# A new order of work and of later loads for a fused attention and gated MLP kernel on one core

## The chip, the core and the metric

The kernel runs on one core of one Trainium2 chip. The metric is device time in microseconds (us), the median over several executions. A core has a tensor engine (PE; its weight loads are listed as PEld), a vector engine (DVE), a scalar engine (ACT), a GpSimd engine (POOL) and a sync engine (SP). Here POOL issues nearly all loads and stores, SP issues the DMA transposes and the last stores. Each engine, and each of these DMA queues, works through its own list in order; semaphores hold an instruction until what it needs is there.

## The reference

```python
# q, k, v: (8, 8, 576, 64); beacon_k, beacon_v: (8, 8, 16, 64)
k_all = np.concatenate([beacon_k, k], axis=2)
v_all = np.concatenate([beacon_v, v], axis=2)
scores = q @ k_all.transpose(0, 1, 3, 2) / 8
causal[:, 16:] = np.triu(np.ones((576, 576), bool), k=1)   # the beacons are seen by all
a = softmax(np.where(causal, -1e9, scores))
x = (a @ v_all).transpose(0, 2, 1, 3).reshape(4608, 512)
out = ((x @ w1) * (x @ w2)) @ w3 @ w_out                    # w1, w2: 512x1024, w3: 1024x1024, w_out: 1024x512
```

Inputs and output are float32.

## The kernel before

The work is in float16 with float32 sums in PSUM. Two facts shape it. First, w3 and w_out are multiplied once into Wt (1024 x 512), so that the MLP is two products per token and one behind them. Second, there is no loop: the program is a list of 1,190 small steps, written out by hand or by a search in the string `ORDER` (line 62 on). A step is a name and its arguments; the last lines of the kernel walk the list and call the function of that name. The order in the string is therefore the order of every engine's own list and of every DMA queue. What the functions do not say, the semaphores that the framework adds do.

The steps, by the engine that they use. b is a batch image (0 to 7), c a chunk of 128 rows, t a pair of heads, h a half of the query blocks, g one of 13 groups of score blocks, mc a block of 512 tokens (0 to 8), kf and mt are blocks of 128 columns or tokens. n is always a PSUM bank, D and A name DVE and ACT, P, S and A the queue of a DMA.

Loads: `lq b c`, `lk b c`, `lv b c` load a chunk of q, k, v; `lkb b`, `lvb b` the beacons; `l1 c`, `l2 c` a quarter of w1, w2 (which serves kf 2c and 2c+1); `l3 r` an eighth of w3; `lo a` a quarter of w_out. They are issued by POOL (and cast to float16 on the way), except the first q and k, which come in float32 on SP and ACT.

Transposes of q and k: `cast`, then `tq`, `tk` (PE) and `eq`, `ek` (the copy out of PSUM, on D or A) in images 0 and 1 and most of 2; `Dq`, `Dk` (a DMA transpose on SP) in the rest and later. For w3: `t3 r` (PE), `e3 r` (copy), `f r a` (two products with w_out), `ew r` (copy into Wt). `tn`, `en` do the beacon keys of image 0.

Attention: `s b g n` (PE) writes a group of scores into a pair of banks, `exp b g n` (ACT) takes it out into a ring of 8 slots, `m b t h` (DVE) multiplies the diagonal blocks by a mask, `v b t h n` (PE) multiplies by the values with a column of ones behind them, `n b t h n` (DVE, two instructions: a reciprocal and a product) divides by the sum. `x b i n` and `ex b i e n` transpose the result through PE and a copy; `TX b i` does it by a DMA transpose on SP.

MLP: `a mc kf n` and `b mc kf n` (PE, four matmuls each), `ea` (copy of a on D or A into one of 3 buffers), `eb` (DVE, product), `o mc mt n` (PE, eight matmuls), `eo` (copy out on D or A into one of 8 buffers), `st mc mt` (the store). The last `o` is split into 384 and 128 columns.

`spin k n` issues k matmuls of zeros, to fill PE's time at the start. `consts` writes masks and zeros.

Two of these functions carry lines that the profile names: the four matmuls of `a` and `b` are line 580, the eight of `o` line 601.

```python
def load_rows(b, c, src, dst):          # lq from image 1 on: line 332 is the dma_start
    rows = min(P, S - c * P)
    nc.gpsimd.dma_start(
        dst[:rows, c], src[b, :, ds(c * P, rows), :].rearrange("h s d -> s h d")
    )
```

`lk` and `lv` issue at line 340, `l1` and `l2` at 390, `l3` at 399; `t3` is line 484, `f` 493, `s` 508, `exp` 518, `v` 539, `eb` 595. An image's q, k, v buffers are used again two images later, so a load of image b waits until the readers of image b-2 are done, and everything behind it on POOL waits with it.

Of the kernel before, what the change touches and what calls it, by code (L numbers as in the profile page):

```python
# [75 lines left out]
f 2 0 4; l1 2; ew 5 A 6; s 0 6 0; s 0 7 2; l3 7; exp 0 6 0; t3 1 6; lq 1 1 P; f 2 1 4; e3 1 D 6;
f 2 2 4; exp 0 7 2; lq 1 4 P; f 2 3 4; m 0 2 0; f 1 0 7; lq 1 0 P; ew 2 A 4; f 1 1 7; f 1 2 7;
lk 1 2 P; f 1 3 7; v 0 2 0 6; lk 1 3 P; ew 1 D 7; v 0 0 0 5; n 0 2 0 6; lk 1 4 P; s 0 8 0;
v 0 0 1 7; exp 0 8 0; n 0 0 0 5; s 0 9 2; s 0 10 4; n 0 0 1 7; lv 1 3; exp 0 9 2; v 0 1 0 6;
m 0 2 1; v 0 1 1 7; exp 0 10 4; n 0 1 0 6; l1 0; t3 7 3; tq 1 3 2; n 0 1 1 7; s 0 11 0; s 0 12 4;  # L80
lv 1 1; eq 1 3 A 2; v 0 2 1 6; e3 7 D 3; exp 0 11 0; l2 0; tq 1 1 7; m 0 3 0; f 7 0 3; n 0 2 1 6;
lq 2 1 P; v 0 3 0 2; exp 0 12 4; f 7 1 3; n 0 3 0 2; l1 1; tk 1 2 6; eq 1 1 A 7; f 7 2 3; m 0 3 1;
x 0 4 5; lv 1 2; x 0 0 4; ek 1 2 D 6; ex 0 4 A 5; tk 1 4 7; v 0 3 1 2; ex 0 0 D 4; ek 1 4 A 7;
l2 1; tk 1 3 6; n 0 3 1 2; f 7 3 3; ek 1 3 A 6; lv 1 4; tq 1 4 7; tq 1 0 5; ew 7 D 3; eq 1 4 A 7;
x 0 3 4; x 0 1 6; lq 2 0 P; eq 1 0 A 5; x 0 2 7; ex 0 3 D 4; ex 0 1 A 6; s 1 0 0; s 1 1 2; s 1 2 4;
ex 0 2 D 7; lv 2 0; exp 1 0 0; a 0 0 6; l2 2; exp 1 2 4; m 1 0 0; b 0 0 7; ea 0 0 D 6; lk 2 0 P;
exp 1 1 2; s 1 3 0; s 1 4 4; eb 0 0 7; tq 2 1 6; a 0 1 7; exp 1 3 0; eq 2 1 D 6; l1 3; m 1 0 1;
b 0 1 6; ea 0 1 D 7; l2 3; exp 1 4 4; s 1 5 2; s 1 6 0; s 1 7 4; m 1 1 0; eb 0 1 6; exp 1 5 2;
lk 2 2 P; b 0 3 7; exp 1 7 4; m 1 1 1; lq 2 2 P; v 1 0 1 6; v 1 1 0 3; n 1 0 1 6; lkb 2; exp 1 6 0;
v 1 1 1 5; lk 2 4 P; tq 2 0 4; n 1 1 0 3; v 1 0 0 6; eq 2 0 A 4; b 0 2 2; n 1 1 1 5; lk 2 3 P;  # L90
m 1 2 0; a 0 2 4; n 1 0 0 6; lv 2 3; v 1 2 0 5; ea 0 2 A 4; a 0 3 6; n 1 2 0 5; lk 2 1 P; eb 0 2 2;
ea 0 3 A 6; s 1 8 0; s 1 9 4; s 1 10 2; exp 1 8 0; eb 0 3 7; lq 2 3 P; a 0 7 6; lq 2 4 P;
exp 1 10 2; m 1 2 1; a 0 6 7; ea 0 7 D 6; lkb 3; Dk 2 0; exp 1 9 4; s 1 11 0; s 1 12 2; ea 0 6 D 7;
lq 3 1 P; tk 2 2 6; b 0 6 7; ek 2 2 D 6; exp 1 11 0; lv 2 4; m 1 3 0; lv 2 1; tk 2 4 6; v 1 3 0 5;
exp 1 12 2; eb 0 6 7; Dk 2 3; a 0 5 4; lq 3 2 P; n 1 3 0 5; ek 2 4 A 6; b 0 5 7; m 1 3 1;
ea 0 5 A 4; lv 2 2; v 1 3 1 6; eb 0 5 7; x 1 4 5; tk 2 1 4; n 1 3 1 6; x 1 0 7; lq 3 4 P;
v 1 2 1 3; ex 1 0 D 7; b 0 4 6; lk 3 2 P; ek 2 1 D 4; ex 1 4 D 5; tq 2 2 7; lk 3 1 P; n 1 2 1 3;
tq 2 4 4; b 0 7 5; eq 2 2 A 7; eq 2 4 D 4; lk 3 4 P; x 1 2 7; eb 0 7 5; x 1 1 4; lvb 2; ex 1 2 A 7;
x 1 3 3; Dq 3 1; a 0 4 2; ex 1 1 D 4; ex 1 3 A 3; lv 3 0; tq 2 3 7; ea 0 4 A 2; a 1 3 5; lq 3 3 P;
eq 2 3 D 7; eb 0 4 6; o 0 2 7; Dq 3 2; lvb 3; ea 1 3 A 5; lq 3 0 P; Dq 3 4; s 2 0 0; s 2 1 2;  # L100
s 2 2 4; eo 0 2 D 7; exp 2 0 0; lv 3 4; o 0 1 6; Dk 3 2; exp 2 1 2; m 2 0 0; st 0 2 P; exp 2 2 4;
o 0 0 7; m 2 0 1; Dk 3 1; eo 0 1 D 6; lk 3 3 P; lk 3 0 P; Dk 3 4; s 2 3 0; s 2 4 2; s 2 5 4;
eo 0 0 A 7; exp 2 4 2; lq 5 2 P; v 2 0 0 6; a 1 0 7; n 2 0 0 6; exp 2 5 4; v 2 0 1 3; ea 1 0 D 7;
lq 4 2 P; o 0 3 6; exp 2 3 0; m 2 1 1; Dq 3 3; lk 4 3 P; n 2 0 1 3; m 2 1 0; s 2 6 4; s 2 7 0;
s 2 8 2; lq 4 3 P; eo 0 3 D 6; exp 2 6 4; v 2 1 0 7; Dq 3 0; st 0 3 P; b 1 0 6; n 2 1 0 7;
exp 2 8 2; m 2 2 0; a 1 1 5; lk 4 2 P; eb 1 0 6; exp 2 7 0; v 2 2 0 7; m 2 2 1; b 1 1 6;
ea 1 1 A 5; n 2 2 0 7; lv 3 1; v 2 1 1 4; eb 1 1 6; a 1 2 7; Dk 3 3; n 2 1 1 4; lq 4 0 P; s 2 9 2;
s 2 10 0; s 2 11 4; exp 2 9 2; Dk 3 0; b 1 3 6; st 0 1 P; exp 2 11 4; m 2 3 0; a 1 4 3; eb 1 3 6;
lv 3 2; exp 2 10 0; v 2 3 0 2; m 2 3 1; b 1 4 6; ea 1 4 D 3; ea 1 2 A 7; v 2 2 1 5; n 2 3 0 2;
lq 4 4 P; a 1 6 7; eb 1 4 6; n 2 2 1 5; x 2 4 4; x 2 0 6; ex 2 4 A 4; a 1 5 3; lv 3 3; ex 2 0 D 6;  # L110
ea 1 6 D 7; b 1 6 6; ea 1 5 A 3; lk 5 3 P; s 2 12 0; s 3 0 4; s 3 1 2; eb 1 6 6; lk 4 0 P;
exp 2 12 0; Dq 4 2; b 1 2 7; lk 4 4 P; exp 3 1 2; v 2 3 1 6; Dk 4 2; lkb 4; eb 1 2 7; s 3 2 0;
s 3 3 2; st 0 0 P; exp 3 0 4; m 3 0 1; a 1 7 7; Dq 4 0; n 2 3 1 6; lv 4 4; exp 3 3 2; b 1 7 5;
m 3 0 0; lk 4 1 P; ea 1 7 D 7; Dk 4 3; exp 3 2 0; x 2 3 6; x 2 1 4; m 3 1 0; x 2 2 7; ex 2 3 D 6;
b 1 5 3; ex 2 2 A 7; Dq 4 4; ex 2 1 D 4; lq 4 1 P; eb 1 7 5; a 2 0 6; eb 1 5 3; Dq 4 3; s 3 4 0;
s 3 5 4; s 3 6 2; ea 2 0 A 6; exp 3 4 0; v 3 1 0 7; o 1 0 6; n 3 1 0 7; exp 3 6 2; exp 3 5 4;
m 3 2 0; v 3 0 1 7; eo 1 0 D 6; Dk 4 0; v 3 2 0 3; v 3 0 0 5; n 3 0 1 7; st 1 0 P; o 1 3 6;
n 3 2 0 3; Dk 4 4; n 3 0 0 5; m 3 1 1; s 3 7 0; s 3 8 2; s 3 9 4; lq 6 4 P; exp 3 7 0; eo 1 3 D 6;
a 2 2 7; lv 4 2; exp 3 8 2; v 3 1 1 6; st 1 3 P; ea 2 2 D 7; Dk 4 1; s 3 10 0; s 3 11 2; exp 3 9 4;
n 3 1 1 6; b 2 2 7; m 3 2 1; exp 3 11 2; a 2 3 6; Dq 4 1; m 3 3 0; eb 2 2 7; exp 3 10 0; v 3 3 0 5;  # L120
ea 2 3 D 6; b 2 1 4; lk 6 0 P; n 3 3 0 5; v 3 2 1 7; lq 5 4 P; m 3 3 1; TX 3 0; lk 5 1 P; b 2 0 6;
n 3 2 1 7; lvb 4; a 2 1 5; eb 2 0 6; TX 3 4; lv 4 3; o 1 2 7; ea 2 1 D 5; lv 4 1; eb 2 1 4;
lq 5 0 P; a 2 4 6; eo 1 2 D 7; lv 4 0; b 2 4 5; ea 2 4 D 6; st 1 2 P; o 1 1 7; eb 2 4 5; s 3 12 2;
s 4 0 0; s 4 1 4; eo 1 1 D 7; exp 3 12 2; Dk 5 3; b 2 7 6; st 1 1 P; exp 4 1 4; b 2 3 7; Dq 5 4;
exp 4 0 0; v 3 3 1 3; m 4 0 1; Dq 5 2; a 2 5 5; eb 2 3 7; lv 5 1; n 3 3 1 3; a 2 7 7; ea 2 5 A 5;
lk 5 4 P; Dq 5 0; m 4 0 0; lk 5 0 P; s 4 2 0; s 4 3 2; s 4 4 4; ea 2 7 A 7; exp 4 3 2; lq 5 3 P;
eb 2 7 6; TX 3 3; b 2 5 7; lkb 6; v 4 0 0 6; exp 4 4 4; m 4 1 0; a 2 6 3; TX 3 2; eb 2 5 7;
lk 5 2 P; exp 4 2 0; n 4 0 0 6; v 4 1 0 7; lv 5 0; b 2 6 5; TX 3 1; ea 2 6 D 3; lq 5 1 P;
v 4 0 1 6; n 4 1 0 7; Dk 5 1; lkb 5; s 4 5 0; s 4 6 2; eb 2 6 5; exp 4 5 0; lv 5 3; o 2 2 7;
n 4 0 1 6; Dk 5 4; exp 4 6 2; lv 5 2; m 4 1 1; s 4 7 4; s 4 8 0; s 4 9 2; eo 2 2 A 7; m 4 2 0;  # L130
exp 4 8 0; st 2 2 P; v 4 2 0 6; o 2 0 7; n 4 2 0 6; Dq 5 3; exp 4 7 4; m 4 2 1; exp 4 9 2;
v 4 1 1 6; eo 2 0 D 7; s 4 10 0; s 4 11 4; s 4 12 2; Dk 5 2; n 4 1 1 6; st 2 0 P; exp 4 10 0;
o 2 3 7; m 4 3 0; Dk 6 0; exp 4 11 4; exp 4 12 2; v 4 2 1 6; m 4 3 1; Dq 6 4; b 3 3 5; n 4 2 1 6;
eo 2 3 A 7; a 3 1 4; Dq 5 1; st 2 3 P; v 4 3 1 7; ea 3 1 D 4; Dk 5 0; a 3 4 6; n 4 3 1 7;
v 4 3 0 4; ea 3 4 A 6; TX 4 2; b 3 6 7; n 4 3 0 4; b 3 1 6; TX 4 0; a 3 3 4; eb 3 1 6; a 3 5 3;
# [562 lines left out]
```

## Time and profile before

| | |
|---|---|
| median of 4 runs | 291.82 us (291.66 to 292.3) |
| the profiled execution | 292.3 us; span from its first to its last instruction 290.6 us |
| busy: PE, DVE, ACT, POOL | 283.8, 174.4, 143.3, 133.9 us |
| granted TensorE clock | 1.00 |
| data moved | 39.32 MB read, 9.44 MB written, 168 GB/s over the span |

A span is the time between the first and the last instruction of the program; the time of a run is some 1.7 us longer. A busy time counts an engine's instructions without its waits; matmuls overlap, so that PE can be busy and yet slower than it could be. In the slices of the page the span is cut in 40 equal parts and each digit is a busy share in tenths. A line of a group has the source line, the engine, the operation, out<-in, and the count.

### The profile page before, as it was taken

The page shows a single profiled execution, that of the slowest core. Times are in us where ns is not written, and L with a number is a line of the kernel's source. Part 1 is how long each engine was busy: PE and PEld are TensorE (multiplying, and loading weights), DVE is VectorE, ACT ScalarE, POOL GpSimd, SP SyncE. Part 2 cuts the span into 40 slices and gives each one's busy share as a digit, 9 for nine tenths or more (in the row PEclk, how much of TensorE's full clock was granted, in tenths as well). Part 3 has the DMA queues.
Part 4 walks back from the last instruction along what each step waited for, and adds up shares of the span by engine and source line. Part 5 has one row for each costly group of instructions (what it writes and reads, how often), then busy time and mean ns, then how long its engine had stood idle before and what let it go on. Part 6 is the DMA issues. An engine that isn't in the chain of part 4 may idle for free.

```text
span 290.6 us, 7026 instructions
## 1 busy us (share of the span) xinstructions
PE 283.8 (98%) x2906; PEld 153.7 (53%) x2906; DVE 174.4 (60%) x377; ACT 143.3 (49%) x181; POOL 133.9 (46%) x187
## 2 busy tenths in 40 slices
PE   7999999999999999999999999999999999999994
PEld 2545675565556565555544555555545445444442
DVE  4356686884676788575563586546746746545621
ACT  3574689655665751578124546567191162110201
POOL 8769897798676267391096951820010011000000
PEclk9999999999999999999999999999999999999999
DMA  9999999999999999999999999999340015200034
GB/s 156 200 195 177 172 172 177 172 145 148 169 180 156 165 178 137 187 127 181 180 111 120 205 125 198 114 163 181 62 87 25 36 38 153 72 2 0 0 146 146
DMA packets 154512, 38.93 MB, mean 134 GB/s; under 512 B 144304, under 2 KB 150192, under 8 KB 154480
## 3 DMA queue, kind: packets, MB, share of 16 engines
q0 software_dynamic: 114800, 26.46, 110.6%
q1 hardware_dynamic: 39472, 11.72, 25.8%
q8 instruction: 23, 0.38, 0.6%
q10 hardware_dynamic: 208, 0.29, 0.4%
q14 instruction: 9, 0.07, 0.1%
HBM read 39.32 MB, written 9.44 MB: 168 GB/s over the span
## 4 chain that ended last, share of the span: by engine, by line
PE 90%; DMA 5%; POOL 3%; issue 1%; DVE 0%; POOLq 0%
PE one L580 44%; PE one L601 22%; PE one L539 10%; PE pair L508 9%; DMA xT<-in_moe_w_dram 5%; PE one L493 2%; PE one L428 1%; PE one L565 1%; POOL st L357 1%; PE one L484 1%; POOL xT L399 1%; POOL wo L402 0%; POOL q L332 0%; POOL k L377 0%; POOL b L369 0%
## 5 line engine op out<-in xcount | busy, mean ns | idle before, releaser
L580 PE MATMUL one<-xT,w 128*128 128x512 f16 x576 | 134.4, 379 | 0.0
L518 ACT ACTIVATE ring<-pair 128x1024 f16<-128x1024 f32 x104 | 99.0, 1028 | 32.5 <-PE pair L508 32.2
L580 PEld LDWEIGHTS <-w 128*128 128x128 f16 x576 | 52.5, 98 | 57.7 <-issue 2.5
L601 PE MATMUL one<-Wt,gT 128*128 128x512 f16 (+2 forms) x296 | 66.5, 373 | 0.0
L595 DVE TENSOR_TENSOR gT<-one,asb 128x512 f16<-128x512 f32 x72 | 48.8, 688 | 26.5 <-PE one L580 16.1
L300 ACT ACTIVATE asb<-one 128x512 f32<-128x512 f32 x34 | 20.4, 599 | 67.8 <-PE one L580 49.8
L615 POOL DMA_DIRECT2D out_dram<-st x27 | 15.3, 567 | 77.0 <-DVE st L302 38.5
L601 PEld LDWEIGHTS <-gT 128*128 128x128 f16 x296 | 27.3, 98 | 30.5 <-issue 0.9
L539 PEld LDWEIGHTS <-ring 128*128 128x128 f16 x960 | 35.8, 97 | 11.4 <-issue 1.1
L340 POOL DMA_DIRECT2D va<-in_v_dram x40 | 34.3, 862 | 13.1 <-PE one L539 9.2
L539 PE MATMUL one<-va,ring 128*128 128x65 f16 x960 | 38.4, 193 | 0.0
L340 POOL DMA_DIRECT2D k<-in_k_dram x35 | 29.8, 857 | 11.7 <-DMA kT<-k 9.2
L551 DVE TENSOR_TENSOR x<-one,rd 128x384 f16<-128x384 f32 (+1 forms) x64 | 31.4, 491 | 2.4 <-DVE rd L550 0.2
L302 DVE TENSOR_SCALAR asb<-one 128x512 f32<-128x512 f32 x38 | 26.1, 688 | 10.1 <-PE one L580 9.7
L332 POOL DMA_DIRECT2D q<-in_q_dram x35 | 30.2, 865 | 3.1 <-DMA qT<-q 1.0
L508 PE MATMUL pair<-qT,kT 64*128 64x80 f16 (+4 forms) x736 | 30.2, 225 | 0.0
L302 DVE TENSOR_SCALAR st<-one 128x512 f32<-128x512 f32 (+1 forms) x23 | 15.4, 672 | 20.6 <-PE one L601 20.5
L508 PEld LDWEIGHTS <-kT 64*128 64x128 f16 x736 | 19.9, 95 | 14.2 <-issue 11.9
L528 DVE TENSOR_TENSOR ring<-ring,MD 128x768 f16<-128x768 f16 x32 | 17.7, 552 | 11.0 <-ACT ring L518 11.0
L550 DVE RECIPROCAL rd<-one 128x6 f32<-128x6 f32 (+1 forms) x64 | 11.7, 182 | 14.9 <-PE one L539 14.6
L300 ACT ACTIVATE st<-one 128x512 f32<-128x512 f32 (+1 forms) x14 | 8.3, 596 | 23.9 <-PE one L601 23.7
L528 DVE TENSOR_TENSOR ring<-ring,MX 128x384 f16<-128x384 f16 x32 | 11.3, 353 | 11.7 <-ACT ring L518 11.7
(62 smaller groups left out, 134.4 us busy)
## 6 DMA issues: line engine op xcount, KB each, us to landing
out_dram<-st POOLq DMA_DIRECT2D x27, 256.0 KB, 5.4
q<-in_q_dram POOLq DMA_DIRECT2D x28, 128.0 KB, 7.3
va<-in_v_dram POOLq DMA_DIRECT2D x24, 128.0 KB, 6.9
k<-in_k_dram POOLq DMA_DIRECT2D x21, 128.0 KB, 6.5
xT<-in_moe_w_dram POOLq DMA_DIRECT2D x8, 256.0 KB, 6.4
w<-in_moe_w_dram POOLq DMA_DIRECT2D x8, 256.0 KB, 7.3
out_dram<-st SPq DMA_DIRECT2D x8, 256.0 KB, 2.0
wo<-in_moe_w_out_dram POOLq DMA_DIRECT2D x4, 256.0 KB, 7.0
```

Source lines behind the costliest of these rows:

```text
L300: nc.scalar.activation(dst, src, AF.Copy, scale=by)
L302: nc.vector.tensor_scalar(dst, src, by, None, ALU.mult)
L332: nc.gpsimd.dma_start(dst[:rows, c], src[b, :, ds(c * P, rows), :].rearrange("h s d -> s h d"))
L340: nc.gpsimd.dma_start(dst[ds(p0, rows), c], src[b, :, ds(s0, rows), :].rearrange("h s d -> s h d"))
L508: nc.tensor.matmul(shape(n, "pair")[:, hh, ds(col, w)], kT[ds(hh * 64, 64), t, ts(jt, P)], qT[ds(hh * 64, 64), t, ds(q0, w)],)
L518: nc.scalar.activation(held(b, g)[:, :, 0:GW], shape(n, "pair"), AF.Exp, scale=scale)
L528: nc.vector.tensor_tensor(blk, blk, msk, ALU.mult)
L539: nc.tensor.matmul(pv[:, 2 * at + hh, 0 : D + 1], held(b, g)[:, hh, ds(col, P)], va[:, jt, 2 * t + hh, 0 : D + 1], start=(jt == 0), stop=( ...
L551: nc.vector.tensor_tensor(x16s[b % NB2][:, ds(2 * h, ni), ts(t, P)].rearrange("p i (h d) -> p i h d", h=2), pv[:, 0 : 2 * ni, 0:D].rearran ...
L580: nc.tensor.matmul(bank(n), w12[:, kt, ds(i * DF + kf * P, P)], xT[:, kt, ds(mc * 512, 512)], start=(kt == 0), stop=(kt == NKT - 1),)
L595: nc.vector.tensor_tensor(gTs[mc % 2][:, kf, :], bank(n), asb[slot["asb", (mc, kf)]], ALU.mult)
L601: nc.tensor.matmul(bank(n)[:, 0:w], gTs[mc % 2][:, kf, ts(mt, P)], Wt[:, kf, ds(c0, w)], start=(kf == 0), stop=(kf == NFT - 1),)
```

## The change

Only the string `ORDER` changes. The steps stay the same, with their operands, but for three things: two spins more (24 instead of 22), the other engine for 96 of the casts and copies that may run on either DVE or ACT (of all 176, DVE has 100 before and 96 after), and the split last tile, which is mt 0 of block 7 instead of mt 3. The banks of many steps change too. The first 74 DMAs of POOL keep their order (up to `lvb 2`); the later loads, stores and DMA transposes, and the order of PE's, DVE's and ACT's steps from the start on, are new. The diff replaces 123 lines of the string by 123 others; these are the parts that the prediction speaks of.

```diff
 consts 0; lq 0 0 S; lk 0 0 A; l3 6; consts 1; spin 8 7; lq 1 2 P; l3 4; lo 1; lkb 0 P;
-cast 0 0 q D; lo 0; cast 0 0 k A; spin 3 7; tq 0 0 6; lkb 1; consts 2; eq 0 0 D 6; spin 1 7;
-tk 0 0 7; lq 0 1 P; t3 6 5; ek 0 0 A 7; lk 0 1 P; e3 6 D 5; spin 2 6; tq 1 2 6; l3 3; eq 1 2 D 6;
-spin 3 7; t3 4 7; lvb 0; e3 4 A 7; lo 2; spin 3 6; tn 0 6; en 0 D 6; spin 1 7; s 0 0 0; s 0 1 2;
...
-eq 0 1 A 5; spin 1 0; t3 3 3; lq 0 3 P; m 0 0 1; s 0 3 0; s 0 4 4; l3 5; e3 3 D 3; exp 0 3 0;
-f 6 2 6; lvb 1; f 4 2 7; exp 0 4 4; m 0 1 0; l3 2; tk 1 0 3; f 3 0 2; ek 1 0 D 3; f 3 1 2; t3 0 5;
-lq 0 2 P; f 3 2 2; e3 0 D 5; cast 0 2 k A; lk 1 1 P; s 0 5 0; f 0 0 4; exp 0 5 0; tk 0 2 5; lv 0 4;
-f 4 3 7; f 0 1 4; ek 0 2 A 5; m 0 1 1; l3 1; f 6 3 6; cast 0 3 k D; ew 4 A 7; f 3 3 2; lv 0 0;
-cast 0 3 q D; ew 6 D 6; tq 0 3 5; tk 0 3 7; eq 0 3 A 5; f 0 2 4; ew 3 D 2; lv 1 0; t3 5 6;
-ek 0 3 A 7; f 0 3 4; e3 5 D 6; lv 0 2; ew 0 A 4; t3 2 7; lv 0 3; f 5 0 6; e3 2 D 7; f 5 1 6;
...
-lq 3 1 P; tk 2 2 6; b 0 6 7; ek 2 2 D 6; exp 1 11 0; lv 2 4; m 1 3 0; lv 2 1; tk 2 4 6; v 1 3 0 5;
-exp 1 12 2; eb 0 6 7; Dk 2 3; a 0 5 4; lq 3 2 P; n 1 3 0 5; ek 2 4 A 6; b 0 5 7; m 1 3 1;
...
-eq 2 3 D 7; eb 0 4 6; o 0 2 7; Dq 3 2; lvb 3; ea 1 3 A 5; lq 3 0 P; Dq 3 4; s 2 0 0; s 2 1 2;
-s 2 2 4; eo 0 2 D 7; exp 2 0 0; lv 3 4; o 0 1 6; Dk 3 2; exp 2 1 2; m 2 0 0; st 0 2 P; exp 2 2 4;
-o 0 0 7; m 2 0 1; Dk 3 1; eo 0 1 D 6; lk 3 3 P; lk 3 0 P; Dk 3 4; s 2 3 0; s 2 4 2; s 2 5 4;
...
-n 3 2 1 7; lvb 4; a 2 1 5; eb 2 0 6; TX 3 4; lv 4 3; o 1 2 7; ea 2 1 D 5; lv 4 1; eb 2 1 4;
-lq 5 0 P; a 2 4 6; eo 1 2 D 7; lv 4 0; b 2 4 5; ea 2 4 D 6; st 1 2 P; o 1 1 7; eb 2 4 5; s 3 12 2;
...
+cast 0 0 q A; lo 0; cast 0 0 k D; lkb 1; consts 2; spin 4 7; tq 0 0 6; tk 0 0 7; eq 0 0 D 6;
+lq 0 1 P; ek 0 0 A 7; t3 6 5; lk 0 1 P; e3 6 A 5; spin 2 0; tq 1 2 6; l3 3; eq 1 2 D 6; spin 3 7;
+t3 4 7; lvb 0; e3 4 A 7; lo 2; spin 3 6; tn 0 6; en 0 D 6; spin 1 7; s 0 0 0; s 0 1 2; s 0 2 4;
+lk 1 0 P; exp 0 0 0; f 6 0 7; l3 0; f 6 1 7; lk 0 2 P; exp 0 2 4; m 0 0 0; f 4 0 6; cast 0 1 q D;
+lo 3; f 4 1 6; cast 0 1 k D; exp 0 1 2; tq 0 1 5; lk 0 3 P; tk 0 1 4; ek 0 1 D 4; eq 0 1 A 5;
+spin 1 0; t3 3 3; lq 0 3 P; m 0 0 1; s 0 3 0; s 0 4 4; l3 5; e3 3 A 3; f 6 2 7; lvb 1; exp 0 4 4;
+f 3 0 3; l3 2; tk 1 0 2; f 3 1 3; exp 0 3 0; f 3 2 3; t3 0 5; lq 0 2 P; ek 1 0 A 2; m 0 1 0;
+f 4 2 6; cast 0 2 k D; lk 1 1 P; e3 0 A 5; s 0 5 0; tk 0 2 4; ek 0 2 D 4; exp 0 5 0; spin 2 2;
+f 4 3 6; lv 0 4; f 0 0 5; ew 4 D 6; l3 1; f 0 1 5; cast 0 3 k A; f 0 2 5; m 0 1 1; lv 0 0;
+cast 0 3 q A; tk 0 3 6; f 0 3 5; ek 0 3 D 6; f 6 3 7; lv 1 0; ew 0 A 5; t3 5 4; ew 6 D 7; tq 0 3 6;
+lv 0 2; e3 5 A 4; f 3 3 3; t3 2 7; ew 3 D 3; lv 0 3; eq 0 3 A 6; f 5 0 5; e3 2 D 7; f 5 1 5;
...
+m 0 2 1; tq 1 3 5; v 0 1 1 7; n 0 1 0 6; l1 0; exp 0 10 0; t3 7 4; n 0 1 1 7; s 0 11 2; s 0 12 0;
+lv 1 1; e3 7 A 4; tq 1 1 6; m 0 3 0; v 0 2 1 7; l2 0; eq 1 3 D 5; exp 0 12 0; eq 1 1 D 6;
...
+ek 1 2 A 6; x 0 4 7; lv 1 2; m 0 3 1; tk 1 3 4; tk 1 4 3; ex 0 4 D 7; ek 1 3 A 4; v 0 3 1 2; l2 1;
...
+s 1 2 2; lv 2 0; ex 0 2 D 6; exp 1 0 0; a 0 1 7; exp 1 2 2; m 1 0 0; l2 2; b 0 1 6; ea 0 1 D 7;
...
+exp 1 6 0; m 1 1 1; v 1 0 1 6; a 0 7 7; lk 2 1 P; exp 1 7 2; m 1 2 0; n 1 0 1 6; s 1 9 0; s 1 10 2;
...
+n 1 1 1 6; a 0 6 4; lkb 3; exp 1 10 2; Dk 2 0; n 1 2 0 7; lq 3 1 P; tk 2 2 6; s 1 11 0; s 1 12 2;
+ek 2 2 D 6; ea 0 6 A 4; lv 2 4; n 1 1 0 5; tk 2 4 7; tq 2 2 6; exp 1 11 0; b 0 5 4; lv 2 1;
+ek 2 4 D 7; Dk 2 3; eq 2 2 D 6; exp 1 12 2; b 0 7 7; lq 3 2 P; m 1 3 1; m 1 3 0; b 0 6 6; lv 2 2;
+eb 0 5 4; eb 0 7 7; tk 2 1 5; v 1 3 1 4; eb 0 6 6; v 1 3 0 7; lq 3 4 P; tq 2 0 3; ek 2 1 D 5;
+v 1 2 1 2; eq 2 0 A 3; lk 3 2 P; n 1 3 0 7; b 0 4 6; n 1 3 1 4; lk 3 1 P; tq 2 4 7; x 1 4 5;
+x 1 0 3; eq 2 4 A 7; n 1 2 1 2; a 0 4 4; lk 3 4 P; ex 1 0 A 3; ex 1 4 D 5; lvb 2; Dq 3 1; x 1 2 7;
+ea 0 4 A 4; x 1 1 5; ex 1 2 D 7; x 1 3 3; lv 3 4; tq 2 3 2; ex 1 1 A 5; eb 0 4 6; o 0 0 7;
+ex 1 3 A 3; lq 3 3 P; eq 2 3 D 2; Dq 3 2; lq 3 0 P; s 2 0 0; s 2 1 4; s 2 2 2; eo 0 0 A 7;
+lk 3 3 P; exp 2 1 4; Dq 3 4; a 1 3 6; o 0 1 7; lq 4 4 P; exp 2 0 0; m 2 0 1; ea 1 3 D 6; Dk 3 2;
+exp 2 2 2; m 2 0 0; lk 3 0 P; s 2 3 4; s 2 4 0; s 2 5 2; eo 0 1 D 7; exp 2 3 4; Dk 3 1; a 1 4 6;
...
+TX 3 0; a 2 4 7; eb 2 2 4; o 1 2 5; TX 3 4; ea 2 4 A 7; lk 6 0 P; lv 4 0; a 2 1 7; eo 1 2 D 5;
+lvb 4; o 1 1 4; ea 2 1 A 7; lk 5 3 P; eb 2 1 6; st 1 2 P; b 2 4 6; lv 4 3; eo 1 1 D 4; lv 4 2;
...
+s 4 4 2; s 4 5 0; s 4 6 4; eb 2 5 7; lvb 5; exp 4 4 2; v 4 0 0 6; Dk 5 3; v 4 1 0 7; n 4 0 0 6;
...
+eo 8 1 D 6; st 8 1 S; o 7 0 6 0 384; eo 8 2 A 7; st 8 2 S; eo 7 0 A 6 0 384; st 7 0 S 0 384;
+o 7 0 5 384 128; eo 7 0 D 5 384 128; st 7 0 S 384 128
```

## The prediction

> **What bounds the kernel now.** First the page: its span, the busy times and the forty slices.
>
> ```profile
> span 290.6 us, 7026 instructions
> PE 283.8 (98%) x2906; PEld 153.7 (53%) x2906; DVE 174.4 (60%) x377; ACT 143.3 (49%) x181; POOL 133.9 (46%) x187
> PE   7999999999999999999999999999999999999994
> PEclk9999999999999999999999999999999999999999
> ```
>
> The tensor engine is busy from the second slice to the last, at the full granted clock, and every other engine has 40% of its time free. A busy digit could hide slow matmuls, so the second view is the chain that ended last. Its columns are start, length, what.
>
> ```profile
> 8.38 6.44 DMA xT<-in_moe_w_dram
> 17.21 7.81 DMA xT<-in_moe_w_dram
> 25.68 1.29 PE one L493 x6
> ...
> 245.40 27.67 PE one L580 x128
> 273.06 13.85 PE one L601 x72
> ```
>
> The chain has two parts. Until 25.02 us it is made of loads: the weight rows of l3 2, issued at 17.21, land at 17.21 + 7.81 = 25.02. From there it is matmuls to the end: 128 of L580 in 27.67 us are 0.216 us each, and nowhere in the middle are they slower. The third view, the stretches (PE, PEld, DVE, ACT, POOL busy), says the same: 3.04 us of PE idle before 30 us, none after, until the last store.
>
> ```profile
> 0.00:30.00 30.00, 26.96 (x248) 13.94 (x249) 14.75 (x37) 16.14 (x21) 23.62 (x42) 1.00 1.35 181
> 30.00:60.00 30.00, 29.97 (x465) 19.25 (x464) 22.31 (x56) 23.48 (x31) 25.47 (x33) 1.00 2.02 173
> 270.00:290.60 20.60, 16.90 (x87) 7.98 (x84) 7.12 (x12) 2.52 (x5) 0.00 (x0) 1.00 0.28 103
> ```
>
> The fourth, the timeline, shows where PE still meets loads, and the end.
>
> ```profile
> 25.06 0.45 PEld L484 LDWEIGHTS <-xT 128*128 128x128 f16 x8 [0.56 <-DMA xT<-in_moe_w_dram]
> ...
> 44.64 0.15 PEld L580 LDWEIGHTS <-w 128*128 128x128 f16 x2 [0.28 <-DMA w<-in_moe_w_dram]
> ...
> 285.81 2.00 SPq L615 DMA_DIRECT2D out_dram<-st  x3
> ...
> 286.93 0.29 DVE L302 TENSOR_SCALAR st<-one 128x128 f32<-128x128 f32 x1 [2.78 <-PE one L601]
> ```
>
> So a reordering can gain only in three places: the landing-bound first 25 us, the small waits inside the busy stretch, and the 3.7 us after the last matmul (286.90 to 290.6).
>
> **How much there is to gain inside.** I took each PE step's interval (its first matmul to the next step's first) and the median for each kind of step and of its successor: a or b 0.863, o 1.727, f 0.432, v 0.368 or 0.549, a score group s 0.225 to 0.236, about 0.095 more when PE enters or leaves a run of score groups. Laid end to end from t3 2 at 25.06, before's own order brings the last step to 285.10; the trace has it at 286.29. So all waits after 25 us come to 1.19 us: 0.38 are gathered by 44, 0.53 by 51, 0.71 by 58, 0.84 by 72, and only 0.35 in the remaining 215 us.
>
> **The change, part by part.**
>
> *Floor.* The steps are the same 1,190 but for three things: 24 spins instead of 22 (all before 20.3 us, where PE waits for loads), over half of the casts and the copies out of PSUM moved from DVE to ACT or back (96 of 176), and mt 0 instead of mt 3 as the split last tile. Score groups stand in 40 runs in both orders (26 of three, 12 of two, 2 of one). With the same medians the new order ends 0.05 us earlier: **-0.05**.
>
> *Start, to t3 2.* The POOL queue is the same for its first 74 DMAs. What gates PE here is landings (the trace gives each issue's): l3 6 at 7.24, l3 4 at 9.33, the beacon keys at 10.80, lo 2 at 16.19, lo 3 at 20.90, l3 2 at 25.02. I followed the new order by hand. The q cast moves to ACT (0.83 instead of 0.56 us) and the k cast to DVE: tq 0 0 goes from 5.92 to 6.19, tk 0 0 from 6.51 to 6.45, and both are done before l3 6's t3 at 7.29. e3 3 on ACT (1.01 instead of 0.69) ends at 16.55, f 3 0 comes at 16.67. The last step before t3 2, f 3 3, ends its interval at 24.94, 0.12 us before the landing. The second added pair of spins ends at 20.24, where PE waits for lo 3 until 20.95 anyway: **0**; without that cover the two would cost 0.43. If the 0.12 fails, the excess is paid in full.
>
> The swapped copies could also touch what POOL issues meanwhile. The group of q loads (duration of an issue in ns, minimum/median/maximum):
>
> ```profile
> L332 POOL DMA_DIRECT2D q<-in_q_dram x35: 689/898/942, 2.3 to 185.7; - x35
> ```
>
> The minimum is a 64-row piece; the 128-row pieces all lie between 0.876 and 0.942 us, and the mean is 0.906 where DVE was over 70% busy beside them (12 of them), 0.879 where under 30% (2). So I price the swaps on POOL at 0 (0.03 us for each of some two issues that they lie beside). The Trainium skill, SBUF — State Buffer, "Who interferes with whom", says otherwise: a DVE copy in a two-port mode holds off GpSimd, and with it the descriptors of DMAs issued there. By that rule, as an estimate, the 1.4 us of DVE copies that leave the time before 17.2 us could bring l3 2 forward by as much, and the sum to 290.4; the rows above show no such wait.
>
> *25 to 58 us, loads of the kept 74.* Their landings should repeat. In the new order PE would be at tk 1 4 at 39.88, its keys land at 40.26: 0.42 late with the wake-up. At b 0 1 it would be at 44.16, l2 0 lands at 44.60: 0.50. At a 0 7 it would be at 53.97, and l1 3 lands at 54.53: 0.62 (these are running totals, not added). Before had 0.53 at 51 and 0.71 at 58: about **-0.05** by 58.
>
> *58 to 68 us, DVE.* Before, DVE has room here:
>
> ```profile
> 57.00:68.00 11.00, 11.00 (x133) 6.91 (x132) 8.33 (x21) 6.45 (x10) 10.06 (x15) 1.00 2.48 148
> ```
>
> The new order puts on it from n 1 2 0 to eq 2 3: five n (3 of 0.64, 2 of 0.78), seven small copies of 0.42, two masks (0.55 and 0.36), four eb of 0.69: 10.1 us without a gap, from about 58.2 to 68.3. Behind this queue x 1 1 waits for ex 1 4 and x 1 2 for n 1 2 1. By the durations alone x 1 1 comes up to 0.35 late; before's order, laid the same way, shows such lateness of 0.1 to 0.2 that the trace does not have. So 0 to 0.35, I take 0.2, against 0.13 in before's 58 to 72: **+0.07**.
>
> *After 72 us.* Here loads and DMA transposes are reordered. I compared each one's lead (from its place in the order to the PE step that needs it). The tightest of before, Dk 3 0, landed 1.3 us ahead of s 3 0; its load lk 3 0 now comes two DMAs earlier on POOL: lead +0.8. TX 5 1 had 2.3: +0.4. TX 7 0 had 2.7: 0. Dk 3 3 had 2.3: +2.7. One became tighter: lv 4 2 and lv 4 3 now stand behind st 1 2 on POOL, which waits for eo 1 2. o 1 2 ends at 114.8, eo at 115.5; lk 5 3, st, lv 4 3, lv 4 2 follow at 115.0, 115.7, 116.3, 117.2. The neighbours at 110 to 113 us took 6.5 to 7.4 to land: 124.1, and v 4 0 0 needs it at 126.2. So no load waits, and I keep before's 0.35: **0** (0 to -0.35 below, +0.35 above).
>
> *End.* o, eo on ACT and DVE, two split stores on SP: the same operations: **0**.
>
> Sum: -0.05 + 0 - 0.05 + 0.07 + 0 + 0 = -0.03 us. The profiled execution took 292.30 (span 290.6 and 1.7 around it), 0.48 above the median of 291.82; so an execution like it would take 292.27, and against the median the sum is **291.8 us**.
>
> **Rivals.** *Waits vanish (faster).* If DVE keeps up at 58 to 68 and nothing waits after 72, the 1.19 shrinks to the 0.62 that landings force: -0.57 - 0.05, so 291.2. For it: DVE and ACT have 40 to 50% free. Against: three landing waits are fixed by the kept loads, so this is about the most that there is. *A late load (slower).* The lv 4 2 above decides if its landing takes over 9.0 us. Landings of this kind go that far:
>
> ```profile
> DMA to landing us min/median/max: 3.4/6.5/10.0
> ```
>
> With 10.0 it lands at 127.2 and costs 1.0; with the 11.6 of the slowest DMA transpose, 2.6. In the middle 1.8: 293.6. For it: the row's maximum is from 73 us, where key loads and transposes crowd, and the new order has transposes at 112 to 115 too. Against: the same queue at 110 to 113 took 7.4 at most. *The start slips (slower).* If f 3 3 misses its 0.12 us or l3 2 lands later, everything moves by that; 0.7 gives 292.5. For it: the margin is thin. Against: PE's wait of 0.7 ahead of lo 3 at 20.95 takes up what slips earlier.
>
> **Chances and range.** 0.2% is 0.58 us, about what a measurement of this kernel can tell from no change. My forecast (within 0.58): 0.60. Waits vanish beyond 0.58, or the start's loads land earlier: 0.15. A late load: 0.15. A slipped start or worse DVE queue: 0.10. So faster 0.15, same 0.60, slower 0.25. The forecast's own range is 291.2 to 292.4 (-0.57 and +0.15 + 0.35 on the two stretches, and a little). The range for 8 in 10 takes in part of the late load: 291.1 to 293.2.
>
> **What would show it.** Right: t3 2 starts at 25.06 with a wait for a DMA in front; PE shows no idle in the stretches from 30 to 270; b 0 1 at 44.6 and a 0 7 at 54.6 behind a DMA; the last o starts within 0.5 us of 286.29. Wrong: a DMA releasing PE at v 4 0 0 or at any s or a after 72 us, a PE gap behind DVE at 61 to 67, or l3 2 landing away from 25.0.

## The result, and the profile after

The changed kernel takes 291.35 us (median of 53 runs, 290.67 to 292.38), the kernel before 291.88 us (79 runs, 290.93 to 294.19): a ratio of 0.9979, 95% interval 0.9972 to 0.9987. That is 0.53 us less (0.38 to 0.82 by the interval), about what a measurement can tell from no change. The prediction said 291.8 and no change; its sum was -0.03, so half a microsecond wants explaining.

The page of the profile after (its execution took 290.86 us), the lines that answer to those of before:

```profile
span 289.2 us, 7029 instructions
PE 283.7 (98%) x2908; PEld 154.5 (53%) x2908; DVE 172.3 (60%) x373; ACT 148.5 (51%) x185; POOL 134.1 (46%) x187
PE   8989999999999999999999999999999999999995
PEclk9999999999999999999999999999999999999999
```

PE's busy time is the same (283.7 us, 283.8 before) at the same clock. DVE has 2 us less work, ACT 5 us more. The stretches (PE, PEld, DVE, ACT, POOL busy) show where PE's idle time went:

```profile
0.00:30.00 30.00, 27.69 (x252) 14.93 (x253) 13.18 (x34) 20.04 (x24) 24.32 (x43) 1.00 1.37 183
30.00:60.00 30.00, 30.00 (x456) 19.14 (x455) 22.69 (x59) 23.62 (x30) 25.61 (x33) 1.00 2.02 173
270.00:289.20 19.20, 16.02 (x83) 7.58 (x80) 5.61 (x10) 3.48 (x6) 0.00 (x0) 1.00 0.30 110
```

Before 30 us PE now idles 2.31 us, not 3.04, and behind the last matmul 3.18, not 3.70. The timeline gives the same points as before: t3 2, b 0 1 behind l2 0, and the last copy out of PSUM.

```profile
24.32 0.58 PEld L484 LDWEIGHTS <-xT 128*128 128x128 f16 x8 [0.19 <-DMA xT<-in_moe_w_dram]
24.47 0.61 PE L484 MATMUL one<-ident,xT 128*128 128x128 f16 x8
...
43.98 0.33 PEld L580 LDWEIGHTS <-w 128*128 128x128 f16 x3 [0.44 <-DMA w<-in_moe_w_dram]
...
281.48 5.45 SPq L615 DMA_DIRECT2D out_dram<-st  x5
...
286.06 0.29 DVE L302 TENSOR_SCALAR st<-one 128x128 f32<-128x128 f32 x1 [2.78 <-PE one L601]
```

The last copy comes at 286.06 instead of 286.93. Of the 1.44 us between these two executions, 0.59 is the start (t3 2 at 24.47 instead of 25.06), 0.28 lies between t3 2 and the last copy, and 0.57 behind it: the stores. The start is chance: in a second profile of each kernel t3 2 began at 24.18 before and at 24.70 after. The stores are less clear. Those on SP, "DMA to landing", after and then before:

```profile
DMA to landing us min/median/max: 1.7/2.0/3.3
```

```profile
DMA to landing us min/median/max: 2.0/2.0/4.2
```

Nearly every profile has a store or two of 2.5 to 4.3 us where the rest take about 2.0. Where such a one delays the last landing, the end comes 0.5 to 0.8 us later: from the start of the last o to the last landing it was 3.39 and 3.36 us in two profiles of before, 3.62 in that of first70_new (a hybrid, see below), and 2.81 to 2.83 in all eleven others, of both orders. So both profiles of before have the late end and both of the change have not; that this is chance is likely from the other kernels, not shown.

So the measure for the order is from the start of t3 2 to the start of the last o. It was 261.23 and 261.45 us before (two profiles), 260.94 and 261.44 after. Two pairs of profiles can't settle half a microsecond; the experiments had to take away what is chance.

### The profile page after: what moved, and what is told of

The parts are those of the page before. It is cut to its first block, busy times and chain, and to the rows that moved or that the text cites. A ratio compares the mean times of both kernels' runs of the same rounds, so it can differ in the third digit from the quotient of the medians.

```text
span 289.2 us, 7029 instructions
## 1 busy us (share of the span) xinstructions
PE 283.7 (98%) x2908; PEld 154.5 (53%) x2908; DVE 172.3 (60%) x373; ACT 148.5 (51%) x185; POOL 134.1 (46%) x187
## 4 chain that ended last, share of the span: by engine, by line
PE 92%; DMA 5%; POOL 1%; issue 0%; DVE 0%; POOLq 0%; DVEq 0%
PE one L580 44%; PE one L601 22%; PE one L539 10%; PE pair L508 9%; PE one L493 3%; DMA st<-in_k_dram 2%; DMA wo<-in_moe_w_out_dram 2%; PE one L428 1%; PE one L565 1%; PE one L484 1%; POOL xT L399 1%; PE one L422 0%; POOL q L332 0%; POOL k L340 0%; POOL wo L402 0%
## 5 line engine op out<-in xcount | busy, mean ns | idle before, releaser
L580 PE MATMUL one<-xT,w 128*128 128x512 f16 x576 | 132.8, 379 | 0.0
L300 ACT ACTIVATE asb<-one 128x512 f32<-128x512 f32 x29 | 17.3, 598 | 67.3 <-PE one L580 63.5
L539 PEld LDWEIGHTS <-ring 128*128 128x128 f16 x960 | 34.6, 98 | 9.4 <-issue 1.3
L539 PE MATMUL one<-va,ring 128*128 128x65 f16 x960 | 37.2, 193 | 0.0
L302 DVE TENSOR_SCALAR asb<-one 128x512 f32<-128x512 f32 x43 | 29.5, 688 | 9.8 <-PE one L580 9.3
L302 DVE TENSOR_SCALAR st<-one 128x512 f32<-128x512 f32 (+1 forms) x19 | 12.7, 669 | 21.4 <-PE one L601 21.4
L300 ACT ACTIVATE st<-one 128x512 f32<-128x512 f32 (+1 forms) x18 | 10.7, 594 | 25.9 <-PE one L601 25.9
L550 DVE RECIPROCAL rd<-one 128x6 f32<-128x6 f32 (+1 forms) x64 | 11.7, 183 | 11.3 <-PE one L539 10.1
```

The source lines that it names most:

```text
L300: nc.scalar.activation(dst, src, AF.Copy, scale=by)
L302: nc.vector.tensor_scalar(dst, src, by, None, ALU.mult)
L539: nc.tensor.matmul(pv[:, 2 * at + hh, 0 : D + 1], held(b, g)[:, hh, ds(col, P)], va[:, jt, 2 * t + hh, 0 : D + 1], start=(jt == 0), stop=( ...
L580: nc.tensor.matmul(bank(n), w12[:, kt, ds(i * DF + kf * P, P)], xT[:, kt, ds(mc * 512, 512)], start=(kt == 0), stop=(kt == NKT - 1),)
```

## The experiments

A ratio stands against the kernel before, run beside the experiment. Its median there was 291.98 us (the four runs of the first group), 291.52 (idle matmuls, and loads moved from 25 us on), 292.03 (new_early and new_early_mild) and 291.62 (old_early_mild): medians of different groups can differ by 0.5 us with no cause in the kernel.

**Half of the order at a time, and the changed kernel again.** Three hybrids, each running the steps of one order up to a cut and the rest in the other. first70_new takes the new order for all that stands ahead of s 2 0 0 (near 70 us), then the old:

```diff
 ea 1 3 D 6; lvb 3; lv 3 0;          # end of the new order's steps
+o 0 2 7; eo 0 2 D 7;                # copied out here, its bank is needed
 s 2 0 0; s 2 1 2; s 2 2 4;          # from here the old order
```

> The steps that stand ahead of s 2 0 0 (about 70 us) in the new order, the rest in the old one. Theory A (what was gained lies in the first 70 us, where PE meets loads): -0.4 to -0.6 us against the kernel before, the last o starts as in the changed kernel. Theory B (it lies in the later loads and the later order): within 0.2 us of the kernel before. Theory C (it is only how the loads of an execution land): within 0.2 too, and its profile's end follows its first landing.

It took 293.36 us, ratio 1.0055 (1.0035 to 1.0076): slower than both.

first70_old is the mirror:

```diff
 lq 3 0 P; lv 3 4; o 0 0 7;          # end of the old order's steps
+eo 0 0 A 7;
 s 2 0 0; s 2 1 4; s 2 2 2;          # from here the new order
```

> The mirror image: the old order up to s 2 0 0, the new one behind it. A: within 0.2 us of the kernel before. B: -0.4 to -0.6 us. C: within 0.2.

292.50 us, 1.0027 (1.0013 to 1.0042).

first25_new cuts behind t3 2:

```diff
 ew 3 D 3; lv 0 3; eq 0 3 A 6; e3 2 D 7;   # new order's steps
 f 5 0 6; f 5 1 6; lv 0 1; f 5 2 6;        # from here the old order
```

> Only the steps ahead of the ones that follow t3 2 (about 25 us) in the new order, all others in the old. If the start holds the gain: -0.4 to -0.6 us. If A holds but by the stretch from 25 to 70 us: within 0.2 us. By the prediction's own step for the start: 0, t3 2 starting with the landing of l3 2 or, where that is early, some 0.1 us behind it.

292.06 us, 1.0010 (0.9997 to 1.0024).

The last of this group is the changed kernel itself, once more.

> The changed kernel once more, in the same rounds. All theories but C: -0.3 to -0.7 us against the kernel before. Its first landing (l3 6) tells how much of a profile's end is chance: a second profile with a landing at 7.2 instead of 6.2 us should end some 0.6 us later than the first profile, at 286 for the end of the last matmul.

291.38 us, 0.9982 (0.9966 to 0.9999), against 291.98 for before beside it: the gain repeats, so pure chance (C) is out. Its first landing tells less than expected: l3 6 came 0.42 us later than in the profile after (6.66 and 6.24), the last o 0.73 later (286.14 and 285.41). Theories A and B both missed, and the halves can't decide between them, because a cut costs more than the change brings. The stretches of PE (length, busy), first70_new, first70_old and first25_new in turn:

```profile
25.00:60.00 35.00, 33.92 (x501) 1.00 2.03 172
60.00:72.00 12.00, 11.24 (x139) 1.00 2.35 143
```

```profile
25.00:60.00 35.00, 34.19 (x509) 1.00 2.03 172
60.00:72.00 12.00, 11.41 (x136) 1.00 2.54 140
```

```profile
25.00:60.00 35.00, 34.39 (x509) 1.00 2.03 172
60.00:72.00 12.00, 12.00 (x146) 1.00 2.61 146
```

At the seam a 1 3 lost 0.92 us in the first (its bank was being emptied by eb 0 4 until 68.23, and ex 1 3 ended at 68.47), o 0 0 0.75 in the second, f 5 0 6 0.71 in the third (behind eq 0 3 on bank 6). Besides, single late landings cost 0.97 in the second (lv 0 1 at 32.69, ahead of v 0 0 0) and 1.24 in the first:

```profile
40.78 0.32 PE L422 MATMUL one<-ident,k 80*128 80x80 f16 x4 [1.08 <-DMA k<-in_k_dram]
```

Two things can still be read. From 72 us on, waits grow by 0.36 us wherever the old late order runs (before, first70_new, first25_new) and by 0.22 to 0.23 with the new one (after, changed_again, first70_old). So the late stretch is worth **-0.13 us** (-0.09 to -0.15 with other choices of which steps share a median). And the new order's end hangs on one landing: the last o starts 231.54 us after l1 3 lands in the profile after (285.41 and 53.87) and 231.55 after it in changed_again (286.14 and 54.59). In the profile after, the weights that a 0 7 needs of it are taken up 0.04 us behind the landing:

```profile
53.91 0.33 PEld L580 LDWEIGHTS <-w 128*128 128x128 f16 x3
```

**Landings or the order?** Theory L: after t3 2 the landings of the kept loads set PE's clock, so an order is worth little. Theory O: the order's own waits count. First I made PE late: 12 idle matmuls (2.59 us) behind t3 2, so that loads have landed when PE comes.

```diff
-t3 2 7; lv 0 3; f 5 0 6;                  # old order
+t3 2 7; lv 0 3; spin 12 6; f 5 0 6;
-eq 0 3 A 6; f 5 0 5;                      # new order
+eq 0 3 A 6; spin 12 5; f 5 0 5;
```

> The old order with 12 idle matmuls of 512 columns (12 x 0.216 = 2.6 us) ahead of f 5 0 6, right behind t3 2, so that TensorE arrives 2.6 us later at everything that it waits for up to 55 us. Theory L: the waits for landings vanish, and of the 2.6 us only 1.9 to 2.1 are seen: 293.8 to 294.0 us. Theory O: 294.4 to 294.5.

> The new order with the same 12 idle matmuls ahead of f 5 0 5, right behind t3 2. Theory L: 293.6 to 293.8 us, 0.2 below the old order with them. Theory O: 293.9 to 294.0, 0.5 below the old order with them.

The old order took 293.65 us (6 runs, 293.43 to 294.14; 1.0075, 1.0051 to 1.0098), the new one 293.23 (7 runs, 292.77 to 293.53; 1.0052, 1.0033 to 1.0071): 0.42 apart, near O's 0.5 and twice L's 0.2; with so few runs, resampling them leaves 0.1 to 1.1. Both times lie below what either theory expected. Against the kernel before beside it (291.52), the old order shows 2.13 of the 2.59 us, so some 0.46 was absorbed, which is L's share; the changed kernel was not run beside the new one. The profiles are sharper. Start of t3 2 and last copy, old order, then new (these kernels' line numbers are six lower, L478 for L484):

```profile
24.65 0.34 PE L478 MATMUL one<-ident,xT 128*128 128x128 f16 x3
288.92 0.29 DVE L296 TENSOR_SCALAR st<-one 128x128 f32<-128x128 f32 x1 [2.78 <-PE one L595]
```

```profile
24.34 0.34 PE L478 MATMUL one<-ident,xT 128*128 128x128 f16 x3
288.15 0.29 DVE L296 TENSOR_SCALAR st<-one 128x128 f32<-128x128 f32 x1 [2.78 <-PE one L595]
```

That is 264.27 against 263.81: in this pair, where behind t3 2 no landing holds PE up by more than 0.05 us, the order alone is worth **-0.46 us**. Two profiles of kernels that follow, in which no landing does so either, put it at -0.30 (old_loads_moved, 261.03 from t3 2 to the last o, and new_early_mild, 260.73). By the prediction's method (medians laid end to end) the 0.46 falls into 0.06 of floor, 0.29 up to 72 us and 0.12 behind it. This split hangs on which steps share a median: with other choices the new order's floor comes out 0.1 to 0.2 longer than the old one's and its waits shorter accordingly. Only the sum is measured. The waits are no single step: both orders lose 0.05 to 0.15 us here and there. Where the trace names what ended such a wait, it is a copy or a product out of PSUM (in the old order at s 1 0 0, a 0 1 and s 1 10, in the new at o 0 0); at others (tq 1 4, v 0 2 1 and v 1 2 1 of the new) it names none. By 72 us these add up to 0.63 in the old and 0.34 in the new.

Second, the same question from the loads' side: the loads with time to spare go behind the urgent ones (POOL's queue from its 27th DMA on, shown from the 25th; nothing else changes).

```diff
-l3 1; lv 0 0; lv 1 0; lv 0 2; lv 0 3; lv 0 1; lq 1 3; l1 2; l3 7; lq 1 1; lq 1 4; lq 1 0;
-lk 1 2; lk 1 3; lk 1 4; lv 1 3; l1 0; lv 1 1; l2 0; lq 2 1; l1 1; lv 1 2; l2 1; lv 1 4;
-lq 2 0; lv 2 0; l2 2; lk 2 0; l1 3; l2 3; lk 2 2; lq 2 2; lkb 2; lk 2 4; lk 2 3; lv 2 3; lk 2 1
+l3 1; lv 0 0; lv 0 2; lv 0 3; lv 0 1; lq 1 3; l3 7; lq 1 1; lk 1 2; lk 1 3; lk 1 4; lq 1 0;
+lq 1 4; l1 0; l2 0; lq 2 1; l1 1; l2 1; lv 1 0; lv 1 3; lv 1 1; lv 1 2; lv 1 4; l1 2; l1 3;
+lk 2 0; lkb 2; lk 2 2; lk 2 4; lk 2 3; lq 2 2; l2 2; l2 3; lk 2 1; lq 2 0; lv 2 0; lv 2 3
```

> The new order with 13 loads that have 3 to 23 us to spare (v of images 1 and 2, two blocks of w1 and w2, two of q) put behind the urgent ones, so that l2 0 and l1 3 are issued 4 loads, some 3.5 us, earlier; the order of all other engines is the changed kernel's. Theory L (the landings of the kept loads set TensorE's clock up to 55 us): the delay behind the floor at 72 us falls from 0.74 to 1.23 us to about 0.4, and the time is 290.5 to 291.0 us, 0.4 to 0.9 below the changed kernel. Theory O (the new order itself is shorter, landings are not what counts): same as the changed kernel, 291.2 to 291.6.

291.67 us, 1.0008 (0.9990 to 1.0026). The same in the old order, with l1 1, l1 2 and lq 2 2 later and lq 2 0 earlier, as its steps need them:

```diff
+... lq 1 4; lq 1 0; l1 0; l2 0; lq 2 1; l2 1; lv 1 0; lv 1 3; lv 1 1; lv 1 2; lv 1 4; lq 2 0;
+l1 1; l1 3; lk 2 0; lkb 2; lk 2 2; lk 2 4; lk 2 3; l2 3; l1 2; l2 2; lk 2 1; lq 2 2; lv 2 0; lv 2 3
```

> The same move of loads in the old order. Theory L: its bound, l2 0 ahead of b 0 0, goes as well, so it gains 0.4 to 0.8 against the kernel before (291.1 to 291.5), and what is left between the new and the old order with moved loads is 0.2 us (0.13 after 72 us, 0.05 of floor). Theory O: 291.9 us as before, and the difference to the new order with moved loads stays 0.5.

291.57 us, 0.9998 (0.9979 to 1.0017). Neither gained, and both theories missed: L's gain is absent, and so is O's 0.5 between them: the new order is 0.10 above the old, and resampling the 12 runs of each leaves -0.5 to +0.6. The profiles show the waits up to 58 us down to 0.16 in the new order, from 0.55 and 1.04 (0.51 in the old, from 0.63 and 0.94). But in new_loads_moved, whose profiled execution was the slowest of its 12 (293.56), the loads behind them came late:

```profile
50.00:60.00 10.00, 10.00 (x175) 6.21 (x173) 7.88 (x21) 9.13 (x11) 8.46 (x11) 1.00 3.09 147
60.00:75.00 15.00, 13.69 (x161) 7.57 (x161) 8.73 (x22) 7.63 (x12) 11.63 (x15) 1.00 2.11 144
```

The DMA share from 50 to 60 us (the time of all packets over that of 16 engines; packets overlap, so it can pass 1) was 3.09, where the profiles of before and of the change have about 2.1, and 147 GB/s were moved instead of 170. PE then idled 1.3 us for l2 3, lk 2 1, lq 2 0 and lq 2 4, and the steps behind them came 1.9 us late. Whether the timed runs paid the same is open.

**Loads moved from the start.** new_early keeps the middle and clears the way to t3 2:

```diff
-l3 4; lo 1; lkb 0; lo 0; lkb 1; lq 0 1; lk 0 1; l3 3; lvb 0; lo 2; lk 1 0; ... l3 5; lvb 1; l3 2;
+l3 4; lkb 0; lo 0; lo 1; lq 0 1; lk 0 1; l3 3; lo 2; lkb 1; lk 1 0; ... l3 5; l3 2;
-... lv 0 0; lv 1 0; lv 0 2; lv 0 3; lv 0 1; lq 1 3; l1 2; l3 7;
+... lv 0 0; lvb 0; lv 0 2; lv 0 3; lv 0 1; lq 1 3; l3 7; lvb 1; lv 1 0; l1 2;
```

> The new order with four small loads that have time (lo 1, lkb 1, lvb 0, lvb 1) and two big ones (lv 1 0, l1 2) put behind loads that TensorE waits for ahead of t3 2; nothing else. In the changed kernel the small ones take 0.2 us each between two landings. If the start is set by the landings, l3 2 lands 0.4 to 0.6 us earlier, t3 2 starts 0.3 to 0.5 earlier, and up to 0.4 us of it is seen at the end if the landings of l2 0 and l1 3, which stay where they were, do not take it back: 291.0 to 291.3 us. If these set the clock in the timed runs too (theory L): no gain, 291.4.

290.99 us, 0.9968 (0.9952 to 0.9984). The time is as expected, the step isn't shown: l3 2 landed at 24.05, but t3 2 started at 24.48, as in the profile after, because PE came from f 3 3 only then. The last o was again 231.55 us behind l1 3 (285.35 and 53.80).

new_early_mild has this start and, from 25 us on, loads with time to spare behind l2 0, l2 1 and l1 3, those of image 2 close to their old places:

```diff
+... lk 1 4; lq 1 0; lq 1 4; l1 0; l2 0; lq 2 1; l1 1; l2 1; lvb 1; lv 1 0; lv 1 3; lv 1 1;
+lv 1 2; lv 1 4; l1 2; l1 3; l2 2; lk 2 0; lq 2 0; l2 3; lk 2 2; lq 2 2; lkb 2; lk 2 4; lk 2 3;
+lk 2 1; lv 2 0; lv 2 3
```

> The same start, and from 25 us on the loads with time to spare behind l2 0, l2 1 and l1 3, so that l2 0 is issued 4 loads earlier and l1 3 is too, while those of image 2 keep about their places. Theory L: start and middle both gain, 0.5 to 0.9 us below the changed kernel (290.5 to 290.9). Theory O (the order's own waits, not landings, are what is left): only the start's 0.3, 291.1.

290.88 us, 0.9966 (0.9952 to 0.9981): the lowest median of all kernels here, 1.0 us under before. It lies in L's range and 0.2 below O's, but only 0.11 below new_early beside it, which has the start alone. Its interval overlaps the changed kernel's; the two were not run side by side. Start and end in its profile:

```profile
24.07 0.33 PE L478 MATMUL one<-ident,xT 128*128 128x128 f16 x3
285.45 0.29 DVE L296 TENSOR_SCALAR st<-one 128x128 f32<-128x128 f32 x1 [2.78 <-PE one L595]
```

From one to the other 261.38, with 261.59 and 262.09 in the two of the changed kernel.

old_early_mild gives the old order such loads, with the same moves up to the places its own steps need:

```diff
+... lk 1 4; lq 1 4; lq 1 0; l1 0; l2 0; lq 2 1; l2 1; lvb 1; lv 1 0; lv 1 3; lv 1 1; lv 1 2;
+lv 1 4; lq 2 0; l1 1; l1 3; lk 2 0; l2 3; lk 2 2; lkb 2; lk 2 4; lk 2 3; l1 2; l2 2; lk 2 1; lq 2 2
```

> The old order with its loads moved like those of the fastest kernel so far: the small ones behind the loads ahead of t3 2, and from 25 us on those with time to spare behind l2 0, l2 1 and l1 3, as the old order needs them. If the order itself is worth 0.4 to 0.5 us once loads are out of the way (theory O), the same loads in the old order give 291.3 to 291.4 us, a ratio of 0.998 to the kernel before, against 290.88 and 0.9966 of the new order with them. If the gain over the changed kernel came from loads alone and the orders were equal without landings, 290.9 us and 0.9966. In the profile, from the start of t3 2 to the last o: 261.0 by theory O (261.03 and 261.03 without landings so far), 260.7 by the other.

291.22 us, 0.9985 (0.9969 to 1.0002): 0.34 us above the new order with moved loads, 0.55 by the two ratios. That is again about O's size, but the two were not run side by side and their intervals overlap (0.9952 to 0.9981 and 0.9969 to 1.0002): a hint, no more. From t3 2 to the last o it took 261.58 us, not 261.0: lv 0 1 landed at 31.95 and held v 0 0 0 back by 0.44.

**The kernel before, a second profile.**

> The kernel before, unchanged, for a second profile of the old order. From the start of t3 2 to the start of the last o the old order took 261.23 us, and 263.62 less 2.59 = 261.03 with the idle matmuls; the new one 260.94, 261.44, and 263.16 less 2.59 = 260.57. Theory O: its own waits are the same in each run, and what differs is landings, so 261.0 to 261.6 here, growth after 72 us 0.36 again.

261.45 us (t3 2 at 24.18, last o at 285.63), and 0.36 after 72 us, as expected. Here the old order, too, hangs on a landing: b 0 0 waits for l2 0.

```profile
44.03 0.11 PEld L580 LDWEIGHTS <-w 128*128 128x128 f16 x2 [0.38 <-DMA w<-in_moe_w_dram]
```

The last o follows l2 0's landing by 241.64 us here (43.99) and by 241.69 in the first profile (44.60). l1 3 lands 9.93 us after l2 0 in all of these profiles, so the new order's 231.55 is 241.48 behind l2 0: for equal landings it ends **0.19 us** earlier.

## Why the prediction was right, and where its sum was not

No change was forecast, and the ratio is about 0.2% down, at the edge of what can be told. That it counts as no change is in part luck: the 0.53 us lie just inside the 0.58 that the forecast allowed, and nearer to the rival "waits vanish" (-0.62) than to the sum of -0.03. Its own signs are mixed too: l3 2 landed at 24.28, not near 25.0, and the last o started at 285.41, 0.88 before 286.29 (24.53 and 286.14 in changed_again). By its steps:

*Floor, -0.05.* Laid end to end, the two orders are 260.03 and 259.98 us long. That is the same sum again; no run shows the floor apart from the waits.

*Start, 0.* Held in substance. t3 2 started at 25.06 and 24.18 in the two profiles of before, at 24.47 and 24.70 after; l3 2's landing decides (25.02 and 24.11, 24.28 and 24.53). The thin margin of 0.12 us is real: in both profiles after, l3 2 came a little early and t3 2 started 0.19 and 0.17 behind it. So "t3 2 at 25.06" was wrong as a point, the mechanism was not. The swapped copies moved POOL's issues by no amount that stands out: l3 2 was issued at 17.21 and 16.30 before, at 16.50 and 17.09 after. The two means that the prediction read are closer still over all 28 of the 128-row issues: 0.904 us where DVE was over 70% busy (15 of them), 0.895 under 30% (5).

*25 to 58 us, -0.05.* This step failed, by taking as certain that landings hide the order. In the profile after, the sum is right to 0.1 us: the running totals 0.42 at tk 1 4, 0.50 at b 0 1, 0.62 at a 0 7 came out as 0.41, 0.43 and 0.55. But that cover depends on when loads land. In changed_again the total by 58 us was 1.04, as lv 0 1 (landed at 32.65) held PE up by 0.44 in v 0 0 0, a landing that the prediction did not list. With PE 2.6 us late the same stretch is worth about -0.26 (waits up to 58 us of 0.42 in the old order, 0.16 in the new). I had priced only what the landings leave, not what the order saves when they come early.

*58 to 72 us, +0.07.* The mechanism did not show. The stretch from 58.2 to 68.3, where I had DVE busy without a gap for 10.1 us:

```profile
58.20:68.30 10.10, 10.10 (x126) 6.33 (x122) 7.88 (x21) 5.19 (x9) 9.23 (x12) 1.00 2.84 153
```

DVE is busy 7.88. x 1 2 and x 1 1, which were to come late behind it, did not: in both profiles after, x 1 2 started 0.865 us behind a 0 4 and x 1 1 0.22 behind x 1 2, the usual intervals. The waits of 58 to 72 us are 0.20 and 0.11 before, 0.19 and 0.19 after: the term is 0 to +0.08 by these medians, and -0.05 to -0.17 with other choices of which steps share one.

*After 72 us, 0.* Missed by **-0.13**, inside the bounds that it was given (-0.35 to +0.35). I kept before's 0.35 because no load came later; but what waits there are come from copies out of PSUM (the largest of before, 0.07 us at a 4 2 behind eb 4 1), and another order of the copies is another sum of them. The loads were judged rightly: Dk 3 0's lead went from 1.29 to 3.79 us, and lv 4 2 landed at 120.57, 4.0 us after its issue and 4.9 ahead of v 4 0 0 at 125.48. So the late load, the dangerous rival, did not happen. A landing may count here all the same: in before_again Dk 3 0 landed at 91.30, 0.11 us ahead of s 3 0. Over the 14 profiles its lead is 0.11 to 5.56 us in the old late order and 2.82 to 8.44 in the new. An execution of the old order in which it comes too late is possible; none was caught.

*End, 0.* The operations are the same, with one slow store whose place changes from run to run. Whether it falls on the last stores more often in the old order (three profiles out of seven) than in the new (none of seven) is open.

So the measured terms give -0.19 us where landings bind (floor -0.05, late stretch -0.13, the middle about 0) and -0.30 to -0.46 where they don't. The timed runs say -0.53 (0.38 to 0.82), -0.42 with the idle matmuls (0.1 to 1.1), and with moved loads once +0.10 and once -0.34, neither clear of zero. The first two are nearer the second figure, and only the first is clear of 0.19. All four profiles of the two kernels showed a binding landing, though, so why the timed runs show the full gain is not settled. The slow store may add to it, and so may Dk 3 0. Whether every execution gains is open as well: at the fastest twentieth of the 79 and of the 53 runs the two kernels are 0.5 us apart, as at the medians, but in changed_again's group the fastest spans of the two kernels are equal (289.3 us) and the medians of the spans 0.5 apart. The rival "waits vanish" (291.2) was the right direction: some of the waits went, not all.

## What to carry to other kernels

A wait that hides another is no fixed price: when a landing covers what a reordering saves, work out the sum with the cover and without it, and let both ends into the forecast. To compare two orders of work, make the late engine later by a known amount of idle work, so that loads drop out, and measure from the same step to the same step. Compare medians only of runs taken side by side: one and the same kernel moved by 0.5 us between groups. Halves of two tuned orders don't add: each seam here cost 0.7 to 0.9 us, more than the whole change is worth.

## What the runs showed of the hardware

The program keeps at most eight of POOL's loads and stores under way. In the trace they set eight landing semaphores in turn (numbers 99 to 106), so that each issue from the ninth on has to wait until the one eight places earlier has landed, and none came before that. Where this wait was the last, the issue followed 0.28 to 0.29 us behind (lvb 0, the 11th, at 9.62 behind l3 4, the 3rd, at 9.33; lo 2 at 10.87 behind lo 1 at 10.59; l3 0 at 12.37 behind lo 0 at 12.08, all of the kernel before). No run tells what the chip itself would allow. So an early first landing can be passed on: l3 6 landed at 7.24 in the first profile of before and at 6.24 after, and l2 0, POOL's 43rd load, at 44.60 and 43.94. It need not: changed_again had 6.66 and 44.67. And of the stores on SP, in 12 of the 14 profiles one was slow, by up to 2.3 us, and mostly those right behind it were late with it (4.22, 3.23, 2.48 and 2.25 us in the first profile of before); which one it was changed, and no cause was found.
